# Mixing and expert kernel: the first stage of batches 1 and 2 on other engines and at other steps

## The chip, the cores and the metric

The program runs on one core of a Trainium2 chip. Its engines work side by side: PE (matrix products), VectorE (DVE), ScalarE (ACT), GpSimd (POOL) and the DMA queues, of which SyncE (SP), ScalarE and GpSimd issue transfers. The metric is the device time of one launch in microseconds, the median of several runs. All stage times below are microseconds from the start of the profiled span.

## The reference

The input x has 8 batches of 2496 tokens with 256 channels. The first half takes the real part of a two-dimensional Fourier transform of each batch; the second half is a layer of 8 experts, of which each token uses one:

```python
X = np.fft.fft(x, axis=1)
X = np.fft.fft(X, axis=2)
x = X.real.reshape(8 * 2496, 256)
logits = x @ w_gate
expert_idx = np.argmax(logits, axis=1)
gate_w = softmax(logits)[expert_idx]          # in short
# tokens sorted by expert; for each expert e:
h = np.maximum(x_sorted[lo:hi] @ w1[e], 0.0)  # 256 -> 1024
y_sorted[lo:hi] = h @ w2[e]                   # 1024 -> 256
out = gate_w[:, None] * y                     # back in the order of the tokens
```

All arithmetic is in float32.

## The kernel before

**The transform of a batch.** The 2496 tokens are 104 x 24. The host lays x out so that each third (q = 0, 1, 2) of the 12 column pairs comes as one load of 896 KB, the tile xq: 104 partitions, four columns and their four mirrored partners, 256 channels each. `load` (L295) issues it from SP; there are three xq buffers.

*Fold.* `fold` adds the partners (L321) and folds the channels in half with a sum and a difference (`fold_d`, L310 and L311) and a small copy (L312), all on VectorE, in place. The last third has one special column more (pm0).

*First stage.* `half1` multiplies two of the four columns with a table of waves (PE tile s, 112 x 512), and ScalarE copies the result out of PSUM to the tile t1 (L336). After two halves the third is stored to DRAM, Td (L411). For batch 1 the store is issued by ScalarE, for later ones by SP. `regroup` (L423) reads Td back in another order into the tile t4s, in two halves of 768 and 640 KB. Batch 0 goes another way: `first_whole` works in smaller pieces and stores straight into t4s.

*Second stage.* `second` makes eleven groups (PE tile p from t4s, copied to zz by ScalarE, L449) and from them ten windows of 128 outputs (PE tile p from zz). ScalarE copies two pieces of a window (zs L475, lg L478) and mirrors the rows of the one before (L454); VectorE makes the 2 x 128 rows (L480). A small turn (pr, L442) precedes each half of the groups. PSUM tiles s, p, pr and rk share three buffers.

*Routing.* After each five windows `route` finds each row's expert and its place in the sorted buffer on VectorE (L494 to L525), with a count on PE (rk). Each row tile goes to `waiting`; `send` takes one from there and writes its 128 rows to the buffer Xs in DRAM by an indirect DMA from GpSimd (L238). From batch 1 on, ScalarE and GpSimd first copy and cast the places (L538, L539).

**The experts.** `plan` builds on VectorE a table of which expert's block comes next (L558 to L592). SP reads it, gathers a block of rows from Xs (xb, L606 and L610) once the batch's row tiles have landed, and loads the expert's weights (w_sb, L616 and L618). VectorE transposes the rows (xT, L654), PE makes ph = w1 x, VectorE and ScalarE apply the relu (hT, L908 and L910), PE makes py = h w2, ScalarE scales it (y, L962), and GpSimd writes the rows to the output by an indirect DMA (L238 again). All PE work is recorded under `mm`, line 223; a float32 product leaves two records.

**The order.** Each engine runs its instructions in the order in which the program writes them; Python generators weave that order. Before the experts start, `second(0)` is stepped through, and `PLAN` says at which of its steps the first stage of batch 1 (`early`) takes a step and how many; each step also sends one row tile. Then the loop over batches pulls expert blocks from `experts` and, by a count of ticks, steps from `side`: the plan of the batch before, what is left of `early`, then `mixed(b)`, which weaves `second(b)` with the first stage of batch b + 1. The first expert block's products are called the turn here. In the order built, three of the six halves of batch 2's first stage and five of batch 1's ten windows stand before the turn on PE.

Of the kernel before, what the change touches and what calls it, by code (L numbers as in the profile page):

```python
# [12 lines left out]
F32 = mybir.dt.float32  # L13
BF16 = mybir.dt.bfloat16
I32 = mybir.dt.int32
ALU = mybir.AluOpType
# [4 lines left out]
B, S, D = 8, 2496, 256  # L21
# [166 lines left out]
WARM = 44  # L188
PLAN = {3: 1, 5: 1, 7: 1, 11: 1, 12: 1, 13: 2, 14: 1, 15: 1, 16: 1}
MOST = max(k for now in rounds() for _, k, _ in now)  # L190
# [27 lines left out]
def kernel(ctx: ExitStack, tc, x, w_gate, w1, w2, out):  # L218
# [87 lines left out]

    def fold_d(o, a, n):

        lo, hi = free(a, 1, [D, n], [1, H - 1]), free(a, D - 1, [D, n], [-1, H - 1])
        vec.tensor_tensor(free(o, 1, [D, n], [1, H - 1]), lo, hi, op=ALU.add)  # L310
        vec.tensor_tensor(free(o, H + 1, [D, n], [1, H - 1]), lo, hi, op=ALU.subtract)  # L311
        vec.tensor_copy(free(o, 0, [D, n], [H, 2]), free(a, 0, [D, n], [H, 2]))  # L312

    def fold(xq, q, pm0):

        a, m = xq[:, 0:4], xq[:, 4:8]
        n = 4
        if q == NQ - 1:
            n = 3
            fold_d(pm0, m[:, 3], 1)  # L320
        vec.tensor_tensor(a[:, 0:n], a[:, 0:n], m[:, 0:n], op=ALU.add)  # L321
        yield
        fold_d(m, a, 4)
        yield

    def half1(b, q, half, pm, pm0, t1):
        ps = pm_.tile([NP, 2, D], F32, tag="m", name="s1")
        for i in range(2):
            s = 4 * q + 2 * half + i
            if s < NS - 1:  # L330
                mm(ps[:, i], con["w1"][:, s], pm[:, 2 * half + i])
                continue
            for k, lo, hi in ((NS - 1, 0, H + 1), (NS + 1, H + 1, D)):
                mm(ps[:, i, lo:hi], con["w1"][:, k], pm0[:, lo:hi], True, False)
                mm(ps[:, i, lo:hi], con["w1"][:, k + 1], pm[:, 3, lo:hi], False, True)
        act.copy(t1[:, 2 * half:2 * half + 2], ps[:])  # L336

# [56 lines left out]
    def first(b):  # L394

        pm0 = xp.tile([NA, D], F32, tag="pm0", name="pm0")
        for q in range(NQ + 1):
# [18 lines left out]
            yield  # L416

    base = con["cap"]

# [7 lines left out]

    t4s = cp.tile([128, 2 * HALF, D], F32, name="t4s")
    zz = cp.tile([128, 2, NW * 128], F32, name="zz")

# [117 lines left out]
    def plan(b, size, k, last):  # L548
# [38 lines left out]
        if not last:  # L587
# [4 lines left out]
            vec.scalar_tensor_tensor(nxt[:], n[:], float(size), gone[:], op0=ALU.mult, op1=ALU.add)  # L592
            gone = nxt
        yield
        tabs[b, size, last] = tab

# [26 lines left out]
    class Left:  # L623


        def __init__(self, w1_sb):
            ws = bp.tile([128, 3, F // 2], F32, tag="ws", name="ws", bufs=2)
            o = [ws[:, k] for k in range(3)]
# [371 lines left out]
    def ahead_of(b):  # L1000

        yield from first(b)
        regroup(b, 0)
        regroup(b, 1)
        if b == 1:
            load(b + 1, NQ - 1)

    def mixed(b):

        one, two = (ahead_of(b + 1) if b + 1 < B else iter(())), second(b)  # L1010
        for _ in range(3):
            next(one, None)
            yield
        for k, _ in enumerate(two):
            if k % 2 == 0:
                next(one, None)
            yield
        yield from woven(close(b), one)
        yield from through(b)
# [37 lines left out]
    early = ahead_of(1)  # L1057
    for _ in range(3):
        next(early)
    for k, _ in enumerate(second(0)):  # L1060
        for _ in range(PLAN.get(k, 0)):
            next(early, None)
        send()
    work = experts(todo)
    steps = {b: mixed(b) for b in range(1, B)}
    for b in range(1, B):
# [4 lines left out]
        if b == 1:  # L1071
            side = woven(chain(close(0), through(0)), chain(early, side))
        blocks = [(size, k * size / BIG, halved(b - 1, size)) for size, k, _ in rounds()[b - 1]]
# [76 lines left out]
```

## Time and profile before

| What | us |
|---|---|
| median of 3 runs (1252.57 to 1254.63) | 1253.59 |
| time of the profiled execution | 1256.62 |
| its span, first to last instruction | 1254.8 |
| busy in the span: PE / PEld / VectorE / ScalarE / GpSimd | 1210.5 / 1077.9 / 761.5 / 431.8 / 448.0 |
| mean granted clock of PE | 0.981 |
| first batch 1 input lands, VectorE folds it | 30.23 |
| batch 0's row tiles sent by GpSimd | 46.64 to 74.03 |
| batch 1's t4s lands, PE goes on | 67.22 |
| first gather of expert rows issued | 80.19 |
| the turn | 85.57 |
| share of the chain that ended last: PE / issue / VectorE / DMA | 65% / 17% / 8% / 4% |

The busy share of an engine is an average over stages. The span falls into a front of some 90 us, in which PE waits and runs at a lowered clock for part of the time, and a long remainder in which PE has hardly a gap. A PE record's end is modelled, so its busy time in a stretch says whether it had work, not at what rate. In the rows of stretches shown below the columns are the stretch, its length, then busy time and number of instructions of PE, PEld, DVE, ACT and POOL, the clock granted to PE (1.00 is full), the DMA share and the GB/s moved.

### The profile page before, as it was taken

How to read it: one execution, taken by the hardware profiler on the slowest of the kernel's cores; microseconds unless marked ns; L12 is line 12 of the kernel's file. 1: busy time of each engine (PE TensorE's matmuls, PEld its weight loads, DVE VectorE, ACT ScalarE, POOL GpSimd, SP SyncE). 2: the span in 40 equal slices, each digit the busy share in tenths (PEclk: the TensorE clock that was granted, in tenths of full speed). 3: DMA queues.
4: the chain of work that ended last, by engine and by line, in shares of the span. 5: the costliest groups of instructions: out<-in, count | busy, mean ns of one | idle time of the engine just before them, and what ended most of it. 6: DMA issues, size and time to landing. Idle time of an engine off the chain costs nothing.

```text
span 1254.8 us, 22389 instructions
## 1 busy us (share of the span) xinstructions
PE 1210.5 (96%) x7317; PEld 1077.9 (86%) x7317; DVE 761.5 (61%) x1820; ACT 431.8 (34%) x1168; POOL 448.0 (36%) x531
## 2 busy tenths in 40 slices
PE   7569999999999999999999999999999999999997
PEld 5458888777788899889988899889999999999996
DVE  4745334343556787566865488686888884444663
ACT  2334333333244433434343433432332332222222
POOL 0426336163126421471226612471463241111112
PEclk8779999999999999999999999999999999999998
DMA  8679899873649443763347435443446238788887
GB/s 235 186 257 347 293 310 309 229 255 99 150 154 271 135 141 119 203 217 112 101 129 216 134 115 172 134 156 98 126 134 192 93 114 302 271 282 292 277 285 270
DMA packets 163062, 248.32 MB, mean 198 GB/s; under 512 B 118542, under 2 KB 130200, under 8 KB 143473
## 3 DMA queue, kind: packets, MB, share of 16 engines
q1 hardware_dynamic: 145644, 201.79, 50.8%
q0 software_dynamic: 16080, 42.85, 9.6%
q10 hardware_dynamic: 1221, 2.24, 0.6%
q8 instruction: 59, 0.97, 0.3%
q14 instruction: 58, 0.48, 0.1%
HBM read 193.45 MB, written 53.45 MB: 197 GB/s over the span
## 4 chain that ended last, share of the span: by engine, by line
PE 65%; issue 17%; DVE 8%; DMA 4%; POOL 3%; ACT 2%; SPq 0%; POOLq 0%; DVEq 0%; ACTq 0%
PE py L223 19%; PE a L223 9%; PE c L223 8%; PE ph L223 7%; PE p L223 6%; PE b L223 5%; PE d L223 4%; PE e L223 3%; PE s L223 3%; POOL out_dram L238 3%; DMA xq<-in_x_dram 2%; DVE xT L654 1%; DMA Td<-t 1%; DMA t4s<-Td 1%; DVE y L754 1%
## 5 line engine op out<-in xcount | busy, mean ns | idle before, releaser
L238 POOL DMA_INDIRECT out_dram<-y,ro x163 | 161.6, 991 | 627.6 <-ACT y L750 302.9
L223 PE MATMUL py<-w_sb,hT 128*128 128x256 f32 x1504 | 340.0, 380 | 0.4 <-DVE hT L908 0.4
L223 PEld LDWEIGHTS py<-w_sb,hT 128*128 128x128 f32 x1504 | 281.3, 190 | 37.6 <-issue 1.0
L238 POOL DMA_INDIRECT Xs<-rows,pi x160 | 161.8, 1011 | 87.5 <-POOL pi L539 42.6
L223 PE MATMUL ph<-xT,w_sb 128*128 128x128 f32 (+2 forms) x992 | 170.9, 328 | 4.7 <-DVE ro L863 4.7
L223 PEld LDWEIGHTS ph<-xT,w_sb 128*128 128x128 f32 x992 | 136.6, 192 | 28.7 <-issue 16.8
L480 DVE SCALAR_TENSOR_TENSOR rows<-p,zs 128x129 f32<-128x129 f32 x160 | 48.8, 347 | 128.2 <-ACT lg L478 122.1
L223 PE MATMUL a<-xT,w_sb 128*128 128x256 f32 (+1 forms) x512 | 117.9, 357 | 0.2 <-DVE xT L654 0.2
L908 DVE TENSOR_SCALAR hT<-ph 128x512 f32<-128x512 f32 x43 | 29.7, 691 | 134.5 <-PE ph L223 74.8
L223 PEld LDWEIGHTS a<-xT,w_sb 128*128 128x128 f32 x512 | 88.6, 190 | 10.2 <-DVE xT L654 0.6
L962 ACT ACTIVATE y<-py,xb 128x256 f32<-128x256 f32 x94 | 44.6, 474 | 151.5 <-PE py L223 151.3
L657 ACT ACTIVATE xT<-xT 128x256 f32<-128x256 f32 (+1 forms) x94 | 36.5, 389 | 173.8 <-DVE xT L654 131.9
L706 DVE TENSOR_TENSOR hT<-hT,b 128x512 f32<-128x512 f32 x57 | 39.2, 688 | 75.7 <-PE b L223 49.2
L716 ACT ACTIVATE hT<-a 128x512 f32<-128x512 f32 x57 | 34.0, 597 | 134.2 <-PE a L223 129.7
L539 POOL CAST pi<-due 128x1 int32<-128x1 f32 x140 | 43.8, 313 | 70.2 <-ACT due L538 70.2
L223 PE MATMUL a<-w_sb,hT 128*128 128x128 f32 x528 | 66.0, 276 | 0.0
L223 PEld LDWEIGHTS a<-w_sb,hT 128*128 128x128 f32 x528 | 63.1, 192 | 0.7
L223 PEld LDWEIGHTS p<-table,t4s 120*128 120x128 f32 x352 | 54.4, 205 | 10.9 <-ACT t4s L442 3.4
L223 PE MATMUL p<-table,zz 128*128 128x145 f32 (+1 forms) x320 | 57.1, 302 | 5.0 <-DVE rows L480 2.2
L223 PE MATMUL c<-xT,ws 128*128 128x256 f32 (+1 forms) x256 | 60.3, 362 | 0.8
L223 PE MATMUL p<-table,t4s 120*128 120x120 f32 (+1 forms) x352 | 57.8, 290 | 3.4 <-ACT t4s L442 2.6
L223 PE MATMUL b<-xs,ws 128*128 128x256 f32 (+1 forms) x256 | 58.7, 356 | 0.0
(163 smaller groups left out, 2063.6 us busy)
## 6 DMA issues: line engine op xcount, KB each, us to landing
w_sb<-in_moe_w_dram SPq DMA_DIRECT2D x132, 1024.0 KB
xq<-in_x_dram SPq DMA_DIRECT2D x23, 896.0 KB
xb<-Xs SPq DMA_DIRECT2D x112, 128.0 KB
Td<-t SPq DMA_DIRECT2D x18, 448.0 KB
t4s<-Td SPq DMA_DIRECT2D x7, 768.0 KB
t4s<-Td SPq DMA_DIRECT2D x7, 640.0 KB
xb<-Xs SPq DMA_DIRECT2D x52, 64.0 KB
xb<-Xs SPq DMA_DIRECT2D x88, 32.0 KB
```

The source lines that it names most:

```text
L223: nc.tensor.matmul(o, lhsT=lhsT, rhs=rhs, start=start, stop=stop, **kw)
L238: return unordered(pool.indirect_dma_start(out=dst, out_offset=bass.IndirectOffsetOnAxis(ap=idx, axis=0), in_=rows, in_offset=None, bounds ...
L480: vec.scalar_tensor_tensor(rows[:, k + m, 0:NY], p3[:, 0:NY], zs[:, 0:1], zs[:, 1:], op0=ALU.add, op1=op)
L539: pool.tensor_copy(idx, due[:])
L654: vec.transpose(free(xT[:], 256 * h, [32, n // 32], [BIG, 2], [1, 32]), free(xb, 512 * h, [64, n // 32], [1, 2], [2, 32]))
L657: act.activation(odd, odd, ACTF.Copy, scale=-1.0)
L706: vec.tensor_tensor(h12, h11, b[:], op=add)
L716: act.activation(h11, a[:], ACTF.Relu)
L754: vec.tensor_tensor(o, o, p[:], op=add)
L908: vec.tensor_scalar(o, ph[:], 0.0, None, op0=ALU.max)
L962: act.activation(y[:, i % 2], py[:], ACTF.Copy, scale=meta[:, i, 1:2])
```

## The change

The first stages of batches 1 and 2 get functions of their own.

- Batch 1 (`first_one`): GpSimd folds the thirds q = 0 and 1, in pieces of two columns; VectorE folds the last third, in pieces woven between the products of the second. The first stage's products are copied out of PSUM by VectorE instead of ScalarE. The results are still stored to Td by ScalarE's queue and read back. The load of batch 2's first third follows batch 1's first products; those of the other two thirds follow the reads of t4s on SP's queue (before, the second third's load came before them).
- Batch 2 (`first_two`): GpSimd folds all three thirds, in whole pieces, behind the sends of batch 0's row tiles in its order; ScalarE copies the products as before. All six halves of its first stage stand behind the turn on PE, and four instead of five windows of batch 1 before it.
- `PLAN` gives other steps; with the one taken ahead, batch 1's first stage takes twelve steps before the turn. Four steps of batch 0's block plan now follow `second(0)` at once.
- The scratch tiles ws of the experts become slices of one buffer (`spare`) used in turn, and a block table is marked as present one step earlier.

The two programs have the same products, stores and loads; every engine's order is the same again from some 140 us of the profile on.

```diff
@@ -186,7 +186,7 @@
 SHARE, EARLY, ROOM = 0.6, 0.7, 1.2
 AHEAD = 12
 WARM = 44
-PLAN = {3: 1, 5: 1, 7: 1, 11: 1, 12: 1, 13: 2, 14: 1, 15: 1, 16: 1}
+PLAN = {7: 2, 11: 1, 12: 2, 13: 2, 14: 1, 15: 1, 16: 1, 17: 1}
 MOST = max(k for now in rounds() for _, k, _ in now)
 
 
@@ -304,36 +304,42 @@
                     in_=x[row:row + NP].rearrange("p (c j d) -> p c j d", c=2, d=D)[:, :, 2 * k:2 * k + 2])
                 yield
 
-    def fold_d(o, a, n):
+    def fold_d(o, a, n, eng=vec):
 
         lo, hi = free(a, 1, [D, n], [1, H - 1]), free(a, D - 1, [D, n], [-1, H - 1])
-        vec.tensor_tensor(free(o, 1, [D, n], [1, H - 1]), lo, hi, op=ALU.add)
-        vec.tensor_tensor(free(o, H + 1, [D, n], [1, H - 1]), lo, hi, op=ALU.subtract)
-        vec.tensor_copy(free(o, 0, [D, n], [H, 2]), free(a, 0, [D, n], [H, 2]))
-
-    def fold(xq, q, pm0):
+        eng.tensor_tensor(free(o, 1, [D, n], [1, H - 1]), lo, hi, op=ALU.add)
+        eng.tensor_tensor(free(o, H + 1, [D, n], [1, H - 1]), lo, hi, op=ALU.subtract)
+        eng.tensor_copy(free(o, 0, [D, n], [H, 2]), free(a, 0, [D, n], [H, 2]))
+
+    def fold(xq, q, pm0, eng=vec):
 
         a, m = xq[:, 0:4], xq[:, 4:8]
         n = 4
         if q == NQ - 1:
             n = 3
-            fold_d(pm0, m[:, 3], 1)
-        vec.tensor_tensor(a[:, 0:n], a[:, 0:n], m[:, 0:n], op=ALU.add)
-        yield
-        fold_d(m, a, 4)
+            fold_d(pm0, m[:, 3], 1, eng)
+        eng.tensor_tensor(a[:, 0:n], a[:, 0:n], m[:, 0:n], op=ALU.add)
+        yield
+        fold_d(m, a, 4, eng)
         yield
 
     def half1(b, q, half, pm, pm0, t1):
         ps = pm_.tile([NP, 2, D], F32, tag="m", name="s1")
+        n = NP
+        col = lambda s: con["w1"][:, s]
         for i in range(2):
             s = 4 * q + 2 * half + i
+            o = ps[0:n, i]
             if s < NS - 1:
-                mm(ps[:, i], con["w1"][:, s], pm[:, 2 * half + i])
+                mm(o, col(s), pm[:, 2 * half + i])
                 continue
             for k, lo, hi in ((NS - 1, 0, H + 1), (NS + 1, H + 1, D)):
-                mm(ps[:, i, lo:hi], con["w1"][:, k], pm0[:, lo:hi], True, False)
-                mm(ps[:, i, lo:hi], con["w1"][:, k + 1], pm[:, 3, lo:hi], False, True)
-        act.copy(t1[:, 2 * half:2 * half + 2], ps[:])
+                mm(o[:, lo:hi], col(k), pm0[:, lo:hi], True, False)
+                mm(o[:, lo:hi], col(k + 1), pm[:, 3, lo:hi], False, True)
+        if b == 1:
+            vec.tensor_copy(t1[0:n, 2 * half:2 * half + 2], ps[0:n])
+        else:
+            act.copy(t1[0:n, 2 * half:2 * half + 2], ps[0:n])
 
     ahead = {}
 
@@ -415,6 +421,67 @@
             pm = xq[:, 4:8]
             yield
 
+    def first_one():
+
+        pm0 = xp.tile([NA, D], F32, tag="pm0", name="pm0")
+
+        def folds(q, eng=vec):
+            xq = ahead[1, q]
+            a, m = xq[:, 0:4], xq[:, 4:8]
+            n = 4
+            if q == NQ - 1:
+                n = 3
+                fold_d(pm0[:], m[:, 3], 1, eng)
+                yield
+            for lo in (0, 2):
+                eng.tensor_tensor(a[:, lo:min(n, lo + 2)], a[:, lo:min(n, lo + 2)], m[:, lo:min(n, lo + 2)], op=ALU.add)
+                yield
+            for lo in (0, 2):
+                fold_d(m[:, lo:lo + 2], a[:, lo:lo + 2], 2, eng)
+                yield
+
+        def products(q):
+            pm = ahead.pop((1, q))[:, 4:8]
+            t1 = xp.tile([NP, 4, D], F32, tag="t1", name="t1")
+            for half in range(2):
+                half1(1, q, half, pm, pm0, t1)
+                if half:
+                    act.dma_start(out=Td[1][:, 4 * q * D:4 * (q + 1) * D], in_=t1[:].rearrange("p j d -> p (j d)"))
+                    if not q:
+                        load(2, 0)
+                yield
+
+        for q in range(2):
+            for _ in folds(q, pool):
+                pass
+        yield
+        yield from products(0)
+        yield from woven(folds(2), products(1))
+        yield from products(2)
+        for h in range(2):
+            regroup(1, h)
+        for q in range(1, NQ):
+            load(2, q)
+
+    def first_two():
+
+        pm0 = xp.tile([NA, D], F32, tag="pm0", name="pm0")
+        pms = []
+        for q in range(NQ):
+            xq = ahead.pop((2, q))
+            for _ in fold(xq, q, pm0[:], pool):
+                pass
+            pms.append(xq[:, 4:8])
+        yield
+        for q in range(NQ):
+            t1 = xp.tile([NP, 4, D], F32, tag="t1", name="t1")
+            half1(2, q, 0, pms[q], pm0, t1)
+            yield
+            half1(2, q, 1, pms[q], pm0, t1)
+            nc.sync.dma_start(out=Td[2][:, 4 * q * D:4 * (q + 1) * D], in_=t1[:].rearrange("p j d -> p (j d)"))
+            load(3, q)
+            yield
+
     base = con["cap"]
 
     def regroup(b, h):
@@ -426,6 +493,8 @@
         ahead[b, "t4", h] = t4
 
     t4s = cp.tile([128, 2 * HALF, D], F32, name="t4s")
+    spare = cp.tile([128, 2, 3, F // 2], F32, name="spare")
+    turns = [0]
     zz = cp.tile([128, 2, NW * 128], F32, name="zz")
 
     def second(b):
@@ -591,8 +660,8 @@
             nxt = one("gone", E)
             vec.scalar_tensor_tensor(nxt[:], n[:], float(size), gone[:], op0=ALU.mult, op1=ALU.add)
             gone = nxt
-        yield
         tabs[b, size, last] = tab
+        yield
 
     def fetch_rows(b, size, tab, i, flat=None):
 
@@ -624,7 +693,8 @@
 
 
         def __init__(self, w1_sb):
-            ws = bp.tile([128, 3, F // 2], F32, tag="ws", name="ws", bufs=2)
+            ws = spare[:, turns[0] % 2]
+            turns[0] += 1
             o = [ws[:, k] for k in range(3)]
             a11, a12, a21, a22 = (w1_sb[:, c, k * F // 2:(k + 1) * F // 2] for k in range(2) for c in range(2))
             self.all = a11, a12, o[2], a22, o[0], o[1], a21
@@ -999,20 +1069,21 @@
 
     def ahead_of(b):
 
-        yield from first(b)
+        if b == 1:
+            yield from first_one()
+            return
+        yield from first_two() if b == 2 else first(b)
         regroup(b, 0)
         regroup(b, 1)
-        if b == 1:
-            load(b + 1, NQ - 1)
 
     def mixed(b):
 
         one, two = (ahead_of(b + 1) if b + 1 < B else iter(())), second(b)
-        for _ in range(3):
+        for _ in range(1 if b == 1 else 3):
             next(one, None)
             yield
         for k, _ in enumerate(two):
-            if k % 2 == 0:
+            if k % 2 == 0 and (b > 1 or k > 7):
                 next(one, None)
             yield
         yield from woven(close(b), one)
@@ -1055,12 +1126,16 @@
         else:
             vec.tensor_copy(con["rd"][:, c, to + E:to + 2 * E], pg[:])
     early = ahead_of(1)
-    for _ in range(3):
-        next(early)
+    next(early)
     for k, _ in enumerate(second(0)):
         for _ in range(PLAN.get(k, 0)):
             next(early, None)
         send()
+    closed = close(0)
+    for _ in range(4):
+        next(closed)
+    for _ in early:
+        send()
     work = experts(todo)
     steps = {b: mixed(b) for b in range(1, B)}
     for b in range(1, B):
@@ -1069,7 +1144,7 @@
         side = chain(steps[b], islice(steps.get(b + 1, iter(())), AHEAD))
         ticks = TICKS + AHEAD * (b == 1)
         if b == 1:
-            side = woven(chain(close(0), through(0)), chain(early, side))
+            side = woven(chain(closed, through(0)), side)
         blocks = [(size, k * size / BIG, halved(b - 1, size)) for size, k, _ in rounds()[b - 1]]
         total = sum(k * (15 if seven_ else 16) for _, k, seven_ in blocks)
         open_ = sum(k * (8 if seven_ else 16) for _, k, seven_ in blocks)
```

More of the change, by code (lines that the diff above doesn't have):

```diff
@@ L593, in plan @@
             gone = nxt
+        tabs[b, size, last] = tab
         yield
-        tabs[b, size, last] = tab
     def fetch_rows(b, size, tab, i, flat=None):
```

## The prediction

> **What bounds the kernel now.** I read the page's slices first, then short stretches by engine, the waits of PE, the order of time on each engine around the first expert matmul, and the order of each engine's instructions in the built programs. The slices give PE 9 tenths or more from the fourth on; only the front has holes. Stretches (stretch; PE, PEld, DVE, ACT, POOL busy us; PE clock; DMA share; GB/s):
>
> ```profile
> 36.00:40.00 4.00, 3.83 (x16) 3.68 (x17) 2.07 (x7) 2.19 (x9) 0.00 (x0) 0.51 0.09 27
> 56.00:60.00 4.00, 0.44 (x11) 0.34 (x10) 3.30 (x18) 0.42 (x2) 3.09 (x4) 0.57 0.95 337
> 60.00:64.00 4.00, 0.00 (x0) 0.00 (x0) 3.79 (x18) 0.00 (x0) 3.39 (x3) 0.50 0.45 128
> 68.00:72.00 4.00, 4.00 (x17) 3.56 (x16) 0.35 (x5) 1.30 (x3) 3.09 (x4) 0.50 1.02 347
> 80.00:84.00 4.00, 0.88 (x4) 0.38 (x3) 3.84 (x16) 1.38 (x5) 0.00 (x0) 0.98 0.38 68
> 104.00:108.00 4.00, 4.00 (x29) 3.50 (x28) 2.13 (x10) 1.99 (x7) 2.14 (x3) 1.00 1.03 420
> ```
>
> PE is empty around 60 and 82, runs at half clock after each hole, and is full from about 88. The waits of PE (waiter, releaser, us, times, longest):
>
> ```profile
> PE pr L223 <- DMA t4s<-Td: 10.8, 1, 10.8
> PE ph L223 <- DVE ro L863: 4.7, 1, 4.7
> ```
>
> The first is batch 1's round trip through DRAM, the second the turn (the first expert matmul, ph). What leads to the turn, in time order (start, duration, engine, line, operation [idle before]):
>
> ```profile
> 30.23 1.23 DVE L321 TENSOR_TENSOR xq<-xq 104x1024 f32<-104x1024 f32 x1 [4.74 <-DMA xq<-in_x_dram]
> 45.58 0.17 DVE L523 TENSOR_TENSOR pi<-pf,table 128x10 int32<-128x10 f32 x1
> 46.64 1.03 POOL L238 DMA_INDIRECT Xs<-rows,pi  x1 [29.40 <-DVE rows L480]
> 73.06 0.97 POOL L238 DMA_INDIRECT Xs<-rows,pi  x1 [0.30 <-issue]
> 80.19 1.93 SPq L606 DMA_DIRECT2D xb<-Xs  x4
> 83.91 0.68 DVE L311 TENSOR_TENSOR xq<-xq 104x508 f32<-104x508 f32 x1
> 84.81 0.70 DVE L654 STREAM_TRANSPOSE xT<-xb 128x512 f32<-128x512 f32 x1
> 85.57 3.78 PE L223 MATMUL ph<-xT,w_sb 128*128 128x256 f32 x8 [4.69 <-DVE ro L863]
> ```
>
> Batch 0's places (pi) are known at 45.7; GpSimd then sends 20 tiles of rows in 27.4 us without a break; the gather (xb) waits for the last to land, 6.1 us after it was issued; a fold of batch 2 stands ahead of the transpose; the turn is at 85.57. Afterwards PE loses only 2.6 us to waits up to 330. So two numbers count: when the turn comes, and how much PE work is left at it.
>
> **What the skill says.** "GPSIMD Engine Reference", section 3.1: a two-input f32 add of 2048 columns takes 4497 ns on GpSimd, 2293 on VectorE. The trace agrees at 512 columns: 1295 (L678) against 684 (L356). Section 2.1: the first call of a freshly loaded GpSimd routine may cost some 6 us more. Not seen here: the first L678 add, right after the load of its routine, took 1.47 us; in the changed program that load stands in GpSimd's idle time from 17 to 30. "TensorE: Matmul & The Clock Gate", Part 1: an idle PE falls to half clock and needs about 3.4 us of activity to come back. The trace agrees (0.50 at 60 to 72; the turn's first eight records take 3.78 us against 1.73 warm). "DMA: Bandwidth & Descriptors", section Issuing engines are not separate DMA queues: all issuers share 16 engines, so a tile sent earlier helps only where there is room. Shares of 1.0 from 64 to 76 and 0.09 at 36 to 40 show both.
>
> **The change, part by part.**
>
> *1. Batch 1's folds, q0 and q1, go to GpSimd.* From 4497 and 1295 ns a column costs 2.08 ns and an instruction 0.23 us: 254 columns 0.76 us. A third in halves is 2 x 1.30 + 4 x 0.76 + 2 x 0.25 (small copies, as L539) = 6.1 us. The first third lands at 30.25, so: half done 34.6, whole 36.4, second third 42.5. GpSimd was idle there. Bounds: VectorE's own 2.7 us a third, and twice my price, 12.3.
>
> *2. VectorE is free for batch 0's windows.* The first window's rows waited from 30.0 (lg copied) to 32.8 behind a fold. A window costs ScalarE 0.36 + 0.27 + 0.41 + 0.18 = 1.22 us, with gaps 1.45: rows at 30.0, then to 36.6 for five (one carries the small turn), against 42.3. But the new PSUM copies stand before routing: 2 x 0.69 (as L908, 128x512 from PSUM) plus matching matmuls, routing starts at 38.5. Its 3.6 us put pi at 42.1. GpSimd is done with q1 at 42.5: **sending starts at 42.6, 4.0 earlier**.
>
> *3. The second half does not follow.* VectorE before, from base to base: rows 3.05, folds 3.05, routing 3.6 = 9.7 us busy in 12.1. After: rows 3.05, q2's fold in pieces 0.74 + 0.69 + 0.42 + 1.8 = 3.65, four PSUM copies 2.76, routing 3.6 = 13.1, and about 2 idle, where rows wait for ScalarE. 42.2 + 15.0 = 57.2 for the second ten places (58.0 before). The first ten tiles are gone at 55.7, so GpSimd waits 1.5, then ten at the 1.4 us of before: **last tile out at 71.0 to 71.2 (74.0 before)**.
>
> *4. Batch 1's round trip.* The last store of Td leaves at 55.7 (55.5 before): ScalarE's copies are gone, VectorE's take their place. One input load (q1 of batch 2) no longer lies beside it but behind the t4s reads, so the store may take 3.5 instead of 5.5 us, and t4s lands at 65.5 instead of 67.2. This is not yet the turn: four windows from there are over at about 74.
>
> *5. The turn.* That input load, 0.9 MB or 2.4 us at 370 GB/s, now competes with the last tiles. From 59.3: t4s 1.4, two loads 1.8, weights 2.1, tiles 1.3 = 6.6 MB, 17.9 us, drained at 77.2 (before, by the same count, 77.4). Last tile issued at 70.2 plus 6.1 to 7 to land: gather at 76.3 to 77.2. Then 5.4 us as before, less 0.7 for the fold no longer ahead of the transpose: **turn at 81.9, 3.7 us earlier**.
>
> *6. What is left at the turn.* Before, PE had done three halves of batch 2's first stage and five windows of batch 1 by then, in time that it otherwise idled; after, no half and four windows: 3 x 0.87 + 0.95 = **3.6 us more PE work behind the turn**, all at PE's full rate.
>
> *7. Batch 2's folds on GpSimd* (5.2 + 5.2 + 5.9 = 16.3 us, queued behind the sends: 71 to 87.5). Queued behind them: the casts and sends of batch 1, due about 12 us after the turn (94), and the first out rows. Cover of 6 us; if the folds took twice as long, 10 us of sends would be late, and these have slack until batch 1's blocks start, some 55 us of expert work later. PE wants q0 about 7 us after the turn: ready at 76.
>
> *8. Batch 2's round trip.* Before, 32 + 32 + 16 records cover it (17.7 us), it took 15.2 from store to landing. After, ph and py cover 13.9; the queue ahead of the store is shorter, so I take a stall of 0.3; the bounds are 0 and 2.4.
>
> *9. The rest costs nothing:* the ws tiles become slices of one buffer with the same two turns; the block table is marked a step earlier; each engine's order is the same again from PE's 435th matmul (about 139 us) on, and there PE bounds.
>
> Sum against the profiled execution (span 1254.8, time 1256.6): -3.7 + 3.6 + 0.3 = +0.2. That execution is 3.0 above the median of the runs, which is 1253.6; carried to the median: **1253.8 us**, no measurable change. A measurement of this kernel can tell about 0.2%, 2.5 us.
>
> **The rivals.**
> *Faster (0.34).* The second ten places come in time, because VectorE idles less than 2 us in part 3; sends run through from 42.6 to 70.0, DMA lands them in 6.1, turn at 80.5; PE's later waits (2.6 us of before) shrink since VectorE and ScalarE have less ahead of the experts: -5.1 + 3.6 - 1.5 = -3, up to -6 where the clock wakes earlier: 1249.5. For it: DMA at 0.09 from 36 to 40 and VectorE's 1.97 us of late rows; against: 13.1 us of VectorE in the second half.
> *Slower (0.20): the landing sets the turn.* The place is the gather's wait on the tiles. With the 0.9 MB moved into the saturated stretch, tiles land no earlier than at 80; the turn stays at 84.5 to 85.5 and the 3.6 us are paid in full: +2.5 to +5, say 1257. It decides from a turn later than 82.0: every us is one us lost, and slower than 0.2% from 84.5.
> *GpSimd does not do what the change says (0.08).* It folds at double price beside a busy VectorE, or each slows the other, which no run shows yet: q1 done at 54.8, sends over at 82, turn near 92: +10, 1263.
>
> **Numbers.** No change 0.38, faster 0.34, slower 0.28 (0.20 + 0.08). The likeliest case alone spans 1251.1 to 1256.1. For 8 in 10 I go to the middle of the faster and past the middle of the slower rival: 1248 to 1259.
>
> **What would show it.** Right: first send at 42 to 43.5; a gap of 1 to 2 us between tile 10 and 11; Td stored at 55 to 57; gather at 76 to 78; ph at 81 to 83; GpSimd's 104x512 adds at 1.3 us; PE without a wait over 1 us after the turn. Wrong: sends at 45 or later (GpSimd's price), no gap (part 3), tiles landing over 7.5 us after issue (part 5), pr of batch 2 waiting for t4s (part 8), a send of batch 1 behind folds with experts waiting for rows (part 7).

## The result and the profile after

The changed kernel takes 1260.03 us, median of 21 runs (1255.81 to 1262.66); the kernel before, beside it, 1255.05 (21 runs, 1252.26 to 1262.78). The ratio is 1.003 with a 95% interval of 1.002 to 1.0041: slower by about 3.8 us. In a second comparison it was 1.0048 (1.0032 to 1.0064). The profiled execution took 1260.03 us, its span is 1258.2. A second profile of the changed kernel comes from that second comparison.

The stretches after, of the rows shown before (stretch; PE, PEld, DVE, ACT, POOL busy us; PE clock; DMA share; GB/s):

```profile
36.00:40.00 4.00, 2.02 (x8) 1.25 (x8) 3.37 (x9) 1.15 (x4) 4.00 (x6) 1.00 0.43 94
56.00:60.00 4.00, 2.45 (x20) 2.22 (x18) 3.05 (x14) 0.27 (x1) 1.79 (x2) 0.50 0.41 137
60.00:64.00 4.00, 0.00 (x0) 0.00 (x0) 3.41 (x24) 0.00 (x0) 2.45 (x3) 0.50 0.53 133
68.00:72.00 4.00, 3.64 (x17) 3.67 (x18) 0.00 (x0) 1.20 (x4) 3.08 (x4) 0.50 1.08 395
80.00:84.00 4.00, 0.00 (x0) 0.00 (x0) 0.00 (x0) 0.00 (x0) 3.92 (x6) 0.50 0.97 327
```

Two rows carry the result. From 36 to 40 GpSimd, idle before, is busy throughout. From 80 to 84, where DMA was down to 0.38 before and VectorE and PE had work, nothing runs but GpSimd's folds, and DMA is still at 0.97. The waits of PE (waiter, releaser, us, times, longest) say what for:

```profile
PE pr L223 <- DMA t4s<-Td: 10.4, 2, 9.9
PE ph L223 <- DVE xT L724: 10.2, 1, 10.2
PE rk L223 <- DVE oh L570: 3.1, 1, 3.1
```

The round trip of batch 1 costs 9.9 us instead of 10.8 (11.0 in the second profile), the turn 10.2 instead of 4.7 (9.3 in the second). The third row is batch 0's first routing, at 41 us; before, PE waited 1.2 us for it. PE has run out of work ahead of the turn, and the turn has not come earlier. What leads to it, in time order:

```profile
31.46 2.50 POOL L437 TENSOR_TENSOR xq<-xq 104x512 f32<-104x512 f32 x2 [13.28 <-DMA xq<-in_x_dram]
43.61 0.17 DVE L592 TENSOR_TENSOR pi<-pf,table 128x10 int32<-128x10 f32 x1
80.92 1.93 SPq L675 DMA_DIRECT2D xb<-Xs  x4
85.99 0.71 DVE L724 STREAM_TRANSPOSE xT<-xb 128x512 f32<-128x512 f32 x1 [8.06 <-DMA xb<-Xs]
86.76 3.78 PE L223 MATMUL ph<-xT,w_sb 128*128 128x256 f32 x8 [10.21 <-DVE xT L724]
```

Here batch 1's first third landed 1.2 us later than in the profile of before, in a part that the change doesn't touch. So stages are compared from the first fold of batch 1 (30.23 before, 31.46 here, 29.90 in the second profile of the changed kernel). "Last tile out" is the end of its issue on GpSimd; "work" is the time from the turn to GpSimd's first sum of expert weights (L678 before, L748 after), which lies at 413 us of the profile of before, behind some 330 us in which PE bounds.

| us after the first fold | before | predicted | after | after, second profile |
|---|---|---|---|---|
| places of the first half (end of pi) | 15.5 | 11.9 | 12.3 | 13.2 |
| places of the second half | 27.8 | 27.0 | 28.7 | 28.4 |
| last tile out | 43.8 | 41.0 | 42.0 | 41.7 |
| first gather | 50.0 | 46.1 to 47.0 | 49.5 | 50.4 |
| turn | 55.3 | 51.7 | 55.3 | 55.0 |
| last tile out to turn | 11.5 | 10.7 | 13.3 | 13.4 |
| work (turn to that sum) | 327.4 | +3.6 | 330.4 | 329.0 |

The turn stands still, and more work lies behind it.

### The profile page after: what moved, and what is told of

Same layout as the page of the kernel before. It is cut to its first block, busy times and chain, and to the rows that moved or that the text cites. A ratio compares the mean times of both kernels' runs of the same rounds, so it can differ in the third digit from the quotient of the medians.

```text
span 1258.2 us, 22430 instructions
## 1 busy us (share of the span) xinstructions
PE 1212.9 (96%) x7317; PEld 1080.7 (86%) x7317; DVE 756.4 (60%) x1807; ACT 428.0 (34%) x1162; POOL 473.7 (38%) x562
## 4 chain that ended last, share of the span: by engine, by line
PE 82%; DVE 8%; DMA 5%; ACT 2%; issue 2%; SPq 1%; POOL 0%; POOLq 0%; DVEq 0%; ACTq 0%
PE py L223 23%; PE ph L223 11%; PE a L223 11%; PE c L223 10%; PE p L223 6%; PE b L223 6%; PE d L223 5%; PE e L223 4%; PE s L223 3%; DMA t4s<-Td 1%; DVE xT L724 1%; DMA Td<-t 1%; DMA xq<-in_x_dram 1%; DVE y L824 1%; DMA w_sb<-in_moe_w_dram 1%
## 5 line engine op out<-in xcount | busy, mean ns | idle before, releaser
L223 PE MATMUL ph<-xT,w_sb 128*128 128x128 f32 (+2 forms) x992 | 171.2, 328 | 10.2 <-DVE xT L724 10.2
L724 DVE STREAM_TRANSPOSE xT<-xb 128x512 f32<-128x512 f32 (+1 forms) x91 | 56.2, 630 | 8.1 <-DMA xb<-Xs 8.1
L223 PE MATMUL c<-xT,spare 128*128 128x256 f32 (+1 forms) x256 | 60.3, 362 | 0.8
```

The costliest lines, as they stand in the source:

```text
L223: nc.tensor.matmul(o, lhsT=lhsT, rhs=rhs, start=start, stop=stop, **kw)
L724: vec.transpose(free(xT[:], 256 * h, [32, n // 32], [BIG, 2], [1, 32]), free(xb, 512 * h, [64, n // 32], [1, 2], [2, 32]))
```

## The experiments

Theory: the turn gained nothing because the load of 0.9 MB that the change moved lies between the last tile and the gather, and because VectorE's places come late; the PE work moved behind the turn is then paid in full. Rivals: the tiles land late for their own bunching, whatever the load; or the moved work is hidden, and the loss has another place.

Each run has a kernel before beside it on the same chip, and its ratio is against that one. The diffs are against the changed kernel.

**Two parts changed back, one kind of work moved, one load moved further.** These four ran on a chip on which the kernel before took 1282.9 us, some 26 more than on the others. Their profiles show engines that stand for some us without a cause that the profile can name; one row of PE's waits in the first is this, which the profiles of the other chips have with 0.2 us at most:

```profile
PE c L223 <- DVE hT L781: 9.1, 4, 2.9
```

These four decide less than the later ones.

The early load:

```diff
-                    if not q:
-                        load(2, 0)
+                    if q < 2:
+                        load(2, q)
@@
-        for q in range(1, NQ):
-            load(2, q)
+        load(2, 2)
```

> One part is undone: the load of batch 2's second third stands again in front of the reads of t4s on SP's queue, as in the kernel before, so that 0.9 MB move at about 50 us and not at 63 us. Theory A (the moved load takes 2.4 us at 370 GB/s from the stretch in which the last row tiles land): the last tile lands about 6 us after its issue and not 8.2, the first gather is at 78.5 instead of 80.9, the turn at 84.4 instead of 86.8, and the time falls by 2.4 us to a ratio of 0.998 against the changed kernel, 1.001 against the one before. Theory B (the tiles land late because they are issued late and bunched, not for want of DMA room): the store of Td and t4s are up to 2 us later, the gather and the turn stay within 0.5 us of 80.9 and 86.8, ratio against before 1.003 or more.

Measured: 1.0039 (1.0019 to 1.0059). Theory A held for the last stretch only: last tile out to turn took 11.3 us. But the second half's places came 35.2 us after the first fold. In the order of time on ScalarE one sees why:

```profile
52.31 0.31 ACTq L449 DMA_DIRECT2D Td<-t  x1
54.43 0.29 ACT L517 COPY zz<-p 128x160 f32<-128x160 f32 x1 [3.39 <-remote]
55.92 0.27 ACT L543 COPY zs<-p 128x130 f32<-128x130 f32 x1 [1.20 <-remote]
```

ScalarE stood for 3.4 us in front of a copy, and everything behind it was late. The run was repeated, below.

More PE work ahead of the turn:

```diff
-                for _ in range(12):
+                for _ in range(14):
                     yield 0, False
@@
-            if k % 2 == 0 and (b > 1 or k > 7):
+            if k % 2 == 0 and (b > 1 or k > 5):
```

> Two more steps of batch 1's side work, and batch 2's first products from the sixth step of the second stage on: one more window and the first two halves of batch 2's first stage stand ahead of the turn on PE, where PE otherwise waits 10 us; VectorE's routing of batch 1 comes partly ahead of the turn too. Theory A (what is left at the turn is paid in full): the turn stays at 86.8 within 0.5 us, and 0.95 + 2 x 0.87 = 2.7 us less work lies behind it; PE's wait ahead of the first expert product falls from 10.2 to some 6; the time falls by 2.7 us, ratio against before 1.001. Theory B (that work is hidden later anyway, or it delays the turn): time within 0.5 us of the changed kernel, ratio 1.003.

Measured: 1.001 (0.999 to 1.0029), as theory A has it; but the engines stood here too, and the turn in the profile is 57.5 after the first fold, where theory A has it unmoved. Repeated below.

ScalarE's copies back:

```diff
-        if b == 1:
-            vec.tensor_copy(t1[0:n, 2 * half:2 * half + 2], ps[0:n])
-        else:
-            act.copy(t1[0:n, 2 * half:2 * half + 2], ps[0:n])
+        act.copy(t1[0:n, 2 * half:2 * half + 2], ps[0:n])
```

> One part is undone: the first stage of batch 1 is again copied out of PSUM by ScalarE (six copies of 112x512), the folds stay on GpSimd. Theory A (VectorE's second half is too full because of the copies): VectorE gets back 6 x 0.69 us, routing starts about 1.4 us earlier, the first send is near 43.4 and not 44.7, the gap between the tenth and the eleventh tile closes (2.8 to under 0.5), the last tile is issued near 70.0 and not 72.5. If the turn follows the last issue, it moves 2 us earlier and the time falls by 2; if DMA sets the landing, the last tile waits over 9 us for its landing, and turn and time stay within 0.7 us. Rival: ScalarE, with 0.9 us a copy, delays the rows by as much as VectorE gains; then sends and gap stay.

Measured: 1.003 (1.0006 to 1.0054). The first send is at 42.8 and the last tile out at 71.8, but in this profile batch 1's first third landed early: after the first fold they are 13.2 and 42.2, as in the changed kernel (13.2 and 42.0). The gap between the tenth and the eleventh tile was 3.6 us, not closed, though smaller than in the other three kernels of this chip (5.5 to 8.3). Inconclusive by itself.

The late load:

```diff
-        for q in range(1, NQ):
-            load(2, q)
+        load(2, 1)
@@ first_two: GpSimd folds q = 2 after the first products of batch 2
+                if not q:
+                    load(2, 2)
```

> The load of batch 2's last third (0.9 MB) moves from its place behind the reads of t4s to behind the first products of batch 2, which is after the turn; GpSimd folds this third after it, the other two as in the changed kernel. Theory A (the bytes in the full stretch from 60 to 82 us set the landing): 2.4 us less to move there, the last tile lands 6 us after issue, the first gather is near 78.5 and the turn near 84.4, the time falls by 2.4 unless batch 2's t4s then comes late for PE, which would show as a wait of pr. Theory B (landing is bound by the tiles' own writes): gather and turn stay within 0.5 us, time within 0.5.

Measured: 1.0089 (1.006 to 1.0118), a miss for both theories. The last stretch is 11.8 us, 1.5 less than in the changed kernel where theory A has 2.4; the price is elsewhere. PE's waits between 90 and 150 us:

```profile
PE ph L223 <- issue: 4.3, 1, 4.3
PE ph L223 <- DVE hT L984: 2.8, 1, 2.8
PE s L223 <- POOL xq L312: 2.5, 1, 2.5
```

The last row is the third that comes late: its fold holds PE. The other two are of the kind that this chip showed in all four runs, so how much of the loss is the edit's stays open.

**The same on a chip without these pauses, and edits together.** Four kernels side by side, the kernel before at 1256.73 us.

> The changed kernel once more, beside the next three, so that stages and times are compared on one chip: ratio against before 1.003 (1.002 to 1.004), gap between tile 10 and 11 near 2.8 us, 13.3 us from the end of the last tile's issue to the turn, the turn 55.3 us after batch 1's first fold starts. If the chip of the first four runs alone made the gaps of 3.6 to 8.3 us seen there, the gap here is near 2.8; if it is 4 or more here too, the second half is less stable than one profile showed.

Measured: 1.0048 (1.0032 to 1.0064), gap 1.9 us, 13.4 from last tile out to turn, turn 55.0 after the first fold. So the gaps of 3.6 to 8.3 were that chip's. The profiled execution (1257.9 us) was 4 us faster than the median of these runs, so stages of single profiles are good to a microsecond or so, not better.

> The load of batch 2's second third in front of the reads of t4s again, a second time. In the first run the stretch from the end of the last tile's issue to the turn was 11.3 us (13.3 in the changed kernel), but an idle ScalarE at 52 to 54 us had put the second half 4 us late. Theory A (the moved load lies between the last tile and the turn): that stretch is again 11.3 us, and without the idle ScalarE the turn comes 2 us earlier and the time is 2 us below the changed kernel beside it (ratio 0.998 to it). Theory B (the earlier load disturbs the second half by as much as it frees later): places of the second half 2 us or more later than in the changed kernel, turn and time within 0.5 us of it.

Measured: 1.0014 (1.0005 to 1.0024), 4.3 us below the changed kernel beside it by the ratios, 2.0 below the first comparison. The last stretch is 11.0 us, and the turn is 53.9 after the first fold, 1.2 to 1.4 earlier. Stretches of 1 us, first of the changed kernel beside it:

```profile
79.00:80.00 1.00, 0.00 (x0) 0.00 (x0) 0.00 (x0) 0.00 (x0) 0.94 (x1) 0.50 0.97 406
80.00:81.00 1.00, 0.00 (x0) 0.00 (x0) 0.00 (x0) 0.00 (x0) 1.00 (x2) 0.50 1.06 442
81.00:82.00 1.00, 0.00 (x0) 0.00 (x0) 0.00 (x0) 0.00 (x0) 1.00 (x3) 0.50 0.67 215
```

And with the early load:

```profile
79.00:80.00 1.00, 0.00 (x0) 0.00 (x0) 0.05 (x1) 0.00 (x0) 1.00 (x3) 1.00 0.87 361
80.00:81.00 1.00, 0.00 (x0) 0.00 (x0) 0.00 (x0) 0.00 (x0) 1.00 (x1) 0.84 0.30 123
81.00:82.00 1.00, 0.00 (x0) 0.00 (x0) 0.00 (x0) 0.00 (x0) 0.92 (x2) 0.50 0.20 40
```

Here DMA is quiet by 80.5 although the last tile went out at 74.1; in the changed kernel it is full until 81 although the last tile went out at 71.6. Theory A holds for the last stretch: 2.3 us of it belong to the moved load (0.9 MB at 370 GB/s are 2.4). Nearly half of that is lost again, since the second half's places are about 1 us later (29.6 after the first fold). That this is the load's doing, as theory B has it, is not shown: PE's mean clock from places to places was 0.71 here and 0.95 in the changed kernel beside it, and the first profile of the changed kernel, at 0.71 too, took as long (16.4 us, 16.6 here).

The PE work and ScalarE's copies together:

> Two edits together: the PE work ahead of the turn (one window and two halves of batch 2's first stage more) and batch 1's copies out of PSUM by ScalarE. Theory (both losses are separate: 2.7 us of work left at the turn, and about 2 us of a turn that comes late since VectorE's second half is full): gap between tile 10 and 11 about 1.5 us shorter than in the changed kernel, turn 2 us earlier, 2.7 us less PE work behind it: 4.5 us below the changed kernel, ratio against before 0.999 to 1.000. Rival (an earlier turn is given back as a stall behind it, since batch 2's round trip through DRAM then has too little cover): the second pr waits 1 us or more for t4s, and the time is only 2.7 us below the changed kernel, 1.001.

Measured: 0.9999 (0.9988 to 1.001). The gap is 0.3 us, the last tile out 39.7 after the first fold, the turn 53.3 (1.8 earlier), the work 326.3 (2.7 to 4.1 less). The theory holds, the rival's stall of pr did not come: the time is 6.2 us below the changed kernel beside it and 3.9 below the first comparison by the ratio, against 4.5 expected. VectorE's second half, from places to places, shrank from 15.2 to 12.8 us; four copies of 0.69 are 2.8.

PE's clock has a part in that half. Where it fell after the first routing, the windows came slower. First the changed kernel in the profile with 16.4 us, then this one:

```profile
44.00:48.00 4.00, 3.55 (x13) 2.83 (x12) 1.73 (x8) 1.00 (x4) 2.73 (x3) 0.50 0.22 82
44.00:48.00 4.00, 3.57 (x22) 2.94 (x21) 1.91 (x6) 2.70 (x9) 3.09 (x4) 1.00 0.35 132
```

PE is busy as long in both and does 13 records in the one, 22 in the other.

The same two edits and the early load:

> The same two edits and the early load of batch 2's second third. Theory A (each gain of the last stretch adds up): the end of the last tile's issue to the turn is 2 us shorter than in the kernel without the early load, the time 2 us lower, ratio against before 0.998. Theory B (the early load costs the second half what it frees later): time within 0.5 us of the kernel with two edits.

Measured: 0.9995 (0.9986 to 1.0004), theory B by the time. But its reason was another. The last tile was out at 70.8 and the gather at 77.4; then, in the order of time:

```profile
79.44 1.27 POOL L311 TENSOR_TENSOR xq<-xq 104x508 f32<-104x508 f32 x1
79.51 1.29 DVE L560 TENSOR_TENSOR eq<-lg,mx 128x80 f32<-128x80 f32 x1
81.77 1.80 POOL L321 TENSOR_TENSOR xq<-xq 104x768 f32<-104x768 f32 x1
81.88 1.78 DVE L566 TENSOR_TENSOR oh<-table,v 128x80 bf16<-128x80 f32 x1
83.58 0.70 DVE L720 STREAM_TRANSPOSE xT<-xb 128x512 f32<-128x512 f32 x1
```

Two operations that take 0.24 us elsewhere take 1.29 and 1.78. Each begins just after a fold on GpSimd has begun, and ends with it (79.44 + 1.27 = 80.71 against 80.80; 81.77 + 1.80 = 83.57 against 83.66). The transpose stands behind them on VectorE with no idle time of its own. But the kernel with two edits has the same 1.29 and 1.78 ahead of its transpose, so they are not the difference between the two. In both this routing begins 48.1 to 48.2 us after the first fold, behind the fifth window of batch 1, and it sets the turn in both; the gather is only 0.4 us earlier here (46.3 after the first fold, 46.7 with two edits). So the early load had little to give in this order. To see what GpSimd's folds cost at the turn, the routing has to stand behind the transpose; from this came the last runs.

**VectorE beside GpSimd.** Another chip, the kernel before at 1257.71 us.

> The work of PE ahead of the turn alone (one window and two halves of batch 2's first stage more), a second time, without the idle engines of the first chip. Theory (each us left at the turn is paid): 2.7 us less than the changed kernel, ratio against before 1.001 if the turn stays where it was. But in this order VectorE has batch 1's routing ahead of the transpose, and GpSimd is folding batch 2 then: a second theory expects the transpose and the turn 1 to 2 us later than in the changed kernel, which takes back as much, ratio 1.002 to 1.003.

Measured: 1.0003 (0.9988 to 1.0019). The work behind the turn is 325.9, 3.1 to 4.5 less than in the two profiles of the changed kernel; the turn is 0.8 to 1.0 later after the first fold, behind the same slow routing. Both theories show in the trace: the gain is paid in full, and part of it is taken back. The time doesn't show the second: 1.002 to 1.003 lies above the interval.

Batch 1's second third folded by VectorE again:

```diff
         for q in range(2):
-            for _ in folds(q, pool):
+            for _ in folds(q, vec if q else pool):
                 pass
```

> One part is undone: batch 1's second third is folded by VectorE again (ahead of the first rows), GpSimd folds only the first third. In the changed kernel four operations of the first routing with two inputs or in a fast mode take 0.46, 0.65, 0.76 and 0.69 us beside GpSimd's folds and 0.24, 0.24, 0.23 and 0.17 us without. Theory (VectorE waits while GpSimd adds): here GpSimd is idle from 36, the four take 0.9 us together and not 2.6; VectorE's own folds of 2.7 us come in front, so the first places are known about 1 us later than in the changed kernel. Rival (the four are slow for another reason, for instance their first use): they take 2.5 us here too, and the places come 2.7 us later. The time: up to 1 us above the changed kernel.

Measured: 1.0078 (1.0056 to 1.0101). The four operations, first of the changed kernel, where GpSimd folds until 42.4:

```profile
39.02 0.46 DVE L564 TENSOR_TENSOR eq<-lg,mx 128x80 f32<-128x80 f32 x1
39.52 0.65 DVE L565 TENSOR_TENSOR eq<-eq,table 128x80 f32<-128x80 f32 x1
40.97 0.76 DVE L574 TENSOR_TENSOR lg<-lg,mx 128x80 f32<-128x80 f32 x1
41.65 0.69 DVE L576 TENSOR_SCALAR rows<-table 128x10 f32<-128x10 f32 x1
```

Then with the second third on VectorE, GpSimd idle from 37.8:

```profile
48.51 0.24 DVE L564 TENSOR_TENSOR eq<-lg,mx 128x80 f32<-128x80 f32 x1
48.79 0.24 DVE L565 TENSOR_TENSOR eq<-eq,table 128x80 f32<-128x80 f32 x1
49.70 0.23 DVE L574 TENSOR_TENSOR lg<-lg,mx 128x80 f32<-128x80 f32 x1
49.85 0.17 DVE L576 TENSOR_SCALAR rows<-table 128x10 f32<-128x10 f32 x1
```

2.56 us against 0.88: the theory holds, and the rival, a first use that is slow here too, is out. The expected 1 us later was wrong: the places came 8 us later. VectorE, in its fixed order, waited for the second third to land (34.7) with the first rows behind it, and PE waited for those rows:

```profile
34.73 1.29 DVE L437 TENSOR_TENSOR xq<-xq 104x512 f32<-104x512 f32 x2 [9.49 <-DMA xq<-in_x_dram]
35.94 0.94 DVE L310 TENSOR_TENSOR xq<-xq 104x254 f32<-104x254 f32 x1
37.74 0.41 DVE L310 TENSOR_TENSOR xq<-xq 104x254 f32<-104x254 f32 x1
```

The last two rows are the same operation beside a fold on GpSimd (0.94) and as GpSimd ends (0.41); GpSimd's own took up to 1.18 beside it, and 0.72 alone. The hindrance goes both ways.

Last, the three edits of above with other steps, so that the transpose stands ahead of batch 1's routing on VectorE: 13 instead of 14, and `k > 3` or `k > 4` (k counts here at even numbers, so that `k > 4` acts as the `k > 5` of above):

```diff
-                for _ in range(14):
+                for _ in range(13):
                     yield 0, False
```

> The kernel with all three edits, with the steps set so that VectorE transposes the first expert rows in front of batch 1's routing and not behind it, and the first half of batch 2's first stage stands after two windows; the same PE work lies ahead of the turn. In the kernel with all three edits three operations of that routing took 1.29, 0.53 and 1.78 us beside GpSimd's folds (0.24 otherwise), and the transpose started at 83.6, 6.1 us after the gather. Theory A (GpSimd's folds hold VectorE, and with it the turn): the transpose starts 3.6 to 4.1 us after the gather, the turn comes 2 us earlier, the time falls 2 us below that kernel, ratio against before 0.998. Theory B (the transpose waits for the rows anyway): turn and time within 0.5 us of it, 0.9995. If PE waits for the fold of batch 2's first third ahead of its later windows, up to 1.5 us of the gain is lost.

Measured (`k > 3`): 1.0034 (1.0018 to 1.005), a miss. PE stood 4.2 us in front of a product that needs GpSimd's fold of batch 2's first third, and all windows behind it came late:

```profile
74.49 2.05 PE L223 MATMUL s<-xq,w 104*112 104x256 f32 x4 [4.22 <-POOL xq L312]
85.11 0.61 DVE L545 SCALAR_TENSOR_TENSOR rows<-p,zs 128x129 f32<-128x129 f32 x2 [2.73 <-ACT lg L543]
85.64 0.70 DVE L720 STREAM_TRANSPOSE xT<-xb 128x512 f32<-128x512 f32 x1
```

I had allowed 1.5 us for this.

> As the one before, but with one half of batch 2's first stage ahead of the turn and not two, at its end, so that PE doesn't wait for GpSimd's fold there. Theory A: the turn as early as there or up to 1 us earlier, 0.87 us more PE work behind it, time equal or 0.9 us more, ratio against before 0.998 to 0.999.

Measured (`k > 4`): 0.9987 (0.9975 to 0.9998). The transpose starts 3.6 us after the gather, against 6.1 with all three edits, and waits for the rows alone, as theory A has it:

```profile
79.74 1.92 SPq L671 DMA_DIRECT2D xb<-Xs  x4
83.37 0.71 DVE L720 STREAM_TRANSPOSE xT<-xb 128x512 f32<-128x512 f32 x1 [2.67 <-DMA xb<-Xs]
84.13 3.35 PE L223 MATMUL ph<-xT,w_sb 128*128 128x256 f32 x7 [4.82 <-DVE xT L720]
```

The turn is 52.7 after the first fold, the earliest of all, but only 0.5 earlier than with all three edits: the gather came 2.0 later (48.3 against 46.3), behind a second half of 15.4 us in which PE's mean clock was 0.72, where it was 1.00 there. The routing now behind the turn is slow in its turn: two operations took 1.24 and 1.18 us, and PE waited 1.6 for it. The work behind the turn is 329.2 us, 2.7 more than with all three edits, of which 0.9 is the half left there and 1.6 this wait. It is the one kernel here whose interval lies below 1, by 1.6 us by the ratio. From the kernel with 0.9995 its interval doesn't part, the profiles show no gain over it, and among thirteen comparisons one that misses 1 so narrowly can be chance.

## Why the prediction held in its range and failed at the turn

The forecast was no change, 1253.8, from an earlier turn (-3.7) against more work behind it (+3.6). Carried by the ratio to the 1253.59 of before that the prediction started from, the changed kernel takes 1257.4: inside the 1248 to 1259 given for 8 in 10, outside the 1251.1 to 1256.1 of the likeliest case. The range held because it reached past a rival, not because the forecast's sum was right. The work was right in kind, the turn was not: what came is the rival named the landing, with its place and nearly its 1257, at 0.20. The load that this rival names is 2.3 of the 3.3 to 3.6 us by which the turn missed its forecast; the rest came from a last tile that was itself 0.7 to 1.1 late.

*Part 5, the turn: the step that failed.* It had the landing at 6.1 to 7 us after the last issue, as before, and DMA drained at 77.2. In the trace the gather came 8.4 us after the start of the last tile's issue (7.1 before; 9.7 in the second profile), DMA was full to some 82.5, and last tile out to turn measured 13.3 and 13.4 us where the step has 10.7. The early load alone brings it to 11.0. So the load moved from 50 to 63 us, which the step priced at 2.4 us of traffic and then put into room that was not there, lies nearly in full between the last tile and the turn in that pair of profiles.

The bytes of the sum were right: the mean rate from the read of t4s to the drain, times its length, gives 6.6 MB in both profiles of the changed kernel and 5.7 before. Its start and its rate were not. Full traffic was to begin at 59.3, 29.1 after the first fold, but t4s was read from 62.0, 30.5 after it (30.1 in the second profile), and the share from 60 to 64 was 0.53; and the mean from there was 322 and 309 GB/s where the sum has 370. At 322 the 6.6 MB take 20.5 us instead of 17.9. In the profile of before the same rate was 328 and the drain at 78.5, where the same count gave 77.4. And the lower end of the step's gather, 76.3, added to the start of the last issue a stretch (6.1) that had been counted from its end; the turn was taken from the upper end.

*Part 2, the first half.* The rows came as early as said, and routing started at 38.8 (38.5), after the first fold 0.9 earlier than said. It took 5.0 us and not 3.6: VectorE waits while GpSimd folds. First places were 0.5 and 1.3 us late after the first fold, the first send 0.8 and 1.7. The rival that had "each slows the other" was right on the mechanism and too high by far on the size: 1.7 us in four operations, and GpSimd's own 254 columns at 0.72 to 0.79 us.

The page "SBUF — State Buffer" of the Trainium skill, section SBUF: two separate sides, states this: VectorE and GpSimd share a pair of ports under an exclusive lock. A GpSimd operation takes it, and so does a VectorE operation in a two-port mode, or with two SBUF inputs if the GpSimd operation reads SBUF; whichever starts first holds it for its whole length, and the other waits. The traces agree in kind: in the two pairs shown VectorE's operation ends 0.09 us after the fold. They agree in what is spared: reductions (0.23), the transpose (0.70) and the rows, with one input in PSUM (0.61 for two), keep their time beside folds. Two operations with one input were held as well: L576 above (0.69 against 0.17) and the small cast behind the transpose (L933, 0.99 and 0.94; 0.12 with GpSimd idle, in the kernel with 1.0034). That these run in a two-port mode no trace here shows. I had not priced it: the prediction costed GpSimd's folds at nothing for VectorE.

*Parts 3 and 4.* The second half took 16.4 and 15.2 us from places to places (15.0 predicted), so VectorE's load was sized about right; it started late. What part 3 left out is PE's clock: its mean in that half was 0.71 in the first profile and 0.95 in the second. In the first it fell after PE had stood 3.1 us for the slow routing; the length of such a wait alone doesn't decide it, for the clock stayed at 1.00 after 2.3 us and fell in another kernel after 2.0. The gap was 2.8 and 1.9 us (1.5), the last tile out 0.7 to 1.1 late, and the last Td store 1.3 to 1.8 late after the first fold (58.8 and 56.7; 55.7 predicted). With the copies on ScalarE the half took 12.8 us in the three profiles whose clock stayed at 1.00, but 15.4 at 0.72. So near full clock the copies on VectorE cost 2.4 us, about what part 3 says, and a change without them would be better. The lowered clock cost 1.2 us with the copies on VectorE and 2.6 with them on ScalarE.

*Part 1* was right. A third in halves took 5.5 us (6.1 predicted), the second was done at 42.44 (42.5).

*Part 6* was right in kind. The work grew by 3.0 and 1.6 us in the two profiles (3.6 predicted). Part of the difference is the clock: PE ran at half clock until 92.8, 89.1 and 90.7 us (first profile, second, before), 6.0, 4.1 and 5.1 after the turn. Half of such a stretch is lost. With what is lost so up to GpSimd's sum taken off (3.0, 2.1 and 2.6 us), the work grew by 2.5 and 2.1. Moving 2.7 us of it ahead of the turn took 3.1 to 4.5 from it in the trace, or 2.8 to 3.2 with the half clock taken off, and 3.4 to 5.7 us from the time by the two comparisons of the changed kernel.

*Part 7* was right on GpSimd's queue. The folds ended at 89.0; the first cast of batch 1 at 100.1 waited for the places:

```profile
88.75 0.20 POOL L312 COPY xq<-xq 104x8 f32<-104x8 f32 x1
100.12 0.19 POOL L608 CAST pi<-due 128x1 int32<-128x1 f32 x1 [11.16 <-ACT due L607]
```

It overlooked VectorE beside these folds; that cost little in the changed kernel, whose routing lies behind the turn, but it held the turn in the kernels that have this routing ahead of it.

*Part 8* was right. Batch 2's first pr waited 0.44 us (0.3 predicted).

*The sum.* By the first pair of profiles the turn gives 0.0 and the work costs 3.0, against 5.0 us between the medians (3.8 by the ratio). The profiled execution of before was 1.6 us slower than the median of its 21 runs, the one of after at its median, which explains most of the rest. The second profile gives -0.3 for the turn and 1.6 for the work, 1.3 together, against 6.0 us by its ratio; that execution was 4.2 faster than the median of its kernel, and where the others lose more no trace shows. So the turn that stood still and the longer work behind it are shown; most of what the second comparison measured is in no trace and stays open.

## What to carry to other kernels

When work is moved to GpSimd, price both ends: its own time, and every VectorE operation with two SBUF inputs that is due meanwhile, which may wait for a whole GpSimd instruction (some with one input waited here too); put what VectorE owes to the critical path into stretches in which GpSimd sends or idles. When a load is moved, ask where it goes as well as where it leaves: where DMA is full until the awaited transfer lands, a load put ahead of it is added to the wait, 2.3 us for 0.9 MB here. Count such traffic at the mean rate of the trace, not at its peak. And a point that stands still makes the work moved behind it a loss at full price.

## What the runs showed of the hardware

VectorE's two-input operations of 0.24 us lasted up to 1.8 us beside one GpSimd add of 768 columns, and ended with it. In the changed kernel, row tiles that landed in 2.5 to 4 us while DMA was at 0.2 to 0.6 took 7.6 to 8.7 us when it was full. The same front of a kernel took 12.8 us for batch 0's second half at PE's full clock and 15.4 at a mean of 0.72. And one of the chips ran the same kernel 2.2% slower, with engines standing for some us without a wait that the profile can name; where they stood differed between kernels, so a single profile from it can't be read as an effect of an edit.
